# Twenty joined score stretches, key trees split by level, and a re-planned order in a sparse-attention and feed-forward kernel

## The chip, the cores and the metric

The kernel runs on one core of one Trainium2 chip. A core has five engines, each with a queue of its own that it works through in order: TensorE (PE; its weight loads are shown apart as PEld), VectorE (DVE), ScalarE (ACT), GpSimd (POOL) and SyncE (SP). Semaphores order them against each other. POOL and SP also issue DMAs. The metric is the device time of one execution in microseconds (us).

## What is computed

Chunk-selecting causal attention over 4 batches of 8 heads, 768 tokens, head size 64, followed by a feed-forward network with squared ReLU over the 3072 tokens:

```python
k_chunks = k.reshape(B, H, nc, chunk, D)              # chunk = 32, nc = 24
k_min, k_max = np.min(k_chunks, axis=3), np.max(k_chunks, axis=3)
ub = np.sum(np.maximum(q * k_min, q * k_max), axis=-1)  # a bound of each query and chunk
ub = np.where(causal, ub, -1e9)
top_chunks = np.argsort(ub, axis=-1)[..., -6:]
mask = (chunk of the key is in top_chunks) & causal
attn = softmax(where(mask, q @ k.T / 8, -1e9))
x = attn @ v                                           # 3072 x 512
h = np.maximum(x @ w_in, 0.0)                          # 3072 x 2048
out = h * h @ w_out                                    # 3072 x 512
```

## The kernel before

**The work.** Heads go in pairs: four pairs a batch, sixteen in all, numbered p from 0. The first 128 tokens of each batch attend only to themselves and are done apart (`first_attention`). For the other 640 queries (`NS` = 5 tiles of 128) each pair has two stages.

`stage_a(p)` makes the selection. For batches 0 and 1 keys and queries are transposed on PE (`turn_keys`, `turn_queries`); for batches 2 and 3 (`BY_DMA` = 2) SP does it by DMA transposes (`turn_by_dma`). DVE then takes minimum and maximum of the keys over each chunk: by one reduction (L892) for batches 0 and 1, by a tree of pairwise maxima or minima (`tree`, L857 to L883) for batches 2 and 3, two trees for two pairs. The tree halves the 32 keys of a chunk in five steps: L871 (two instructions), L877 three times, L880. PE multiplies the bounds (`ub`), DVE finds the six best of each query (L805) and marks them (`select`).

`stage_b(p)` is the attention proper. For batches 0 and 1 the marks ride along as 24 more rows of the score product (88 rows instead of 64; L1056). For batches 2 and 3 (p from `RP` = 8 on) `spread` turns the marks into a 0/1 mask: SP transposes them into `sT`, four DMAs write them to DRAM (`rowm`, L1000), four more read them back, spread over partitions, as `keep` (L1005; two buffers), and POOL cuts the diagonal (L669). `stage_b_rows` (L1099) computes these pairs' scores: the 20 tiles of one head fill five PSUM banks (`HEADS`), the two heads of a pair lie in the upper and the lower 64 rows of the array (L1139). Each bank then has an exponential on ACT (L1154), a product with `keep` on DVE (L1157) and four products with the values on PE (L1164). `normalise` divides by the sums (L726, L728) and writes x.

The feed-forward (`ffn`) runs once for the first tiles of all batches and once for each batch, between the attention of the next pairs: `up` (L1231), relu (L1238 on ACT or L1240 on DVE), square (L1252 or L1254), `down` (L1271), a copy `ob<-py` (L398 on ACT or L400 on DVE; three `ob` buffers) and the output DMA on SP (L1285).

**Stretches.** One entry of PE's queue that computes scores of batches 2 and 3 is called a stretch here. `HELD = [(0, 1), (2, 3), (4,)]` (L1027) says which banks of a pair go together: two, two and one, each for both heads. So a pair has three stretches, of four, four and two PSUM banks, and the eight pairs have 24. PSUM buffers: three of tag `ps`, one `tp`, two `av`, two `ff`; a stretch of four banks takes all of `ps` and `tp`.

**What sets the order.** Nothing is scheduled at run time. Every step is entered with `plan.op`, with its possible engines and a cost for each. `ORDER` lists, for each engine, the numbers of the steps in the order of its queue; a step that could run on two engines runs on the one whose list holds it. `Plan.order` walks through these lists with its costs, with a time that a result takes to the next engine (`HAND_OVER`, `BUSY`) and with a small model of the DMAs (`late` is added to a transfer). What comes of that walk is which buffer of a tag a tile gets, how the lists interleave as the program is written, and how many idle matmuls keep PE warm in the first 30 us (`keep_warm`). The walk's costs do not run on the chip; the lists do.

Of the kernel before, what the change touches and what calls it, by code (L numbers as in the profile page):

```python
# [78 lines left out]
class Plan:  # L79
# [7 lines left out]
    HAND_OVER = {"PE": 0.22, "ACT": 0.10, "DVE": 0.10, "POOL": 0.12, "SP": 0.1}  # L87
    BUSY = 0.09
# [27 lines left out]
    def order(self):  # L116
# [10 lines left out]
        landed, done = [], []  # L127
        dma = Transfers()
        at = {e: 0 for e in self.given}
        while len(done) < len(self.ops):  # L130
            found = []
            for engine, line in self.given.items():
# [18 lines left out]
                if op.packets and not op.turns and len(landed) >= 8:  # L151
                    st = max(st, landed[-8].end)
# [16 lines left out]
            if op.packets:  # L169
                dma.add(op)  # L170
                if not op.turns:
                    landed.append(op)
# [27 lines left out]
    def write(self):  # L200
# [47 lines left out]
        1790 1791 1796 1797 1800 1801 1802 1803 1806 1807 1808 1809""",  # L248
    "ACT": """
# [21 lines left out]
        1804 1810""",  # L271
    "DVE": """
# [1093 lines left out]
```

## Time and profile before

| | |
|---|---|
| median of 3 runs | 264.62 us (267.29, 264.62, 264.58) |
| the profiled execution | 266.55 us, its span 264.7 us |
| granted clock of PE | 1.000 |
| DMA packets, bytes | 111124, 37.92 MB |
| idle time of PE ahead of `ph` (L1231), of which most waits for `ob` (L400) | 2.8 us |
| score stretches, L1139 | 24 |
| chain that ended last, by engine | PE 64%, DVE 18%, DMA 6%, ACT 5% |

How to read the lines that follow. In a group of instructions stand line, engine, operation, tile written <- tile read, shapes, count, then busy us, the mean of one in ns, and the idle time of the engine just before, with what ended it. In a timeline stand start and duration in us; x4 means four like instructions drawn together. Matmuls overlap: a matmul's drawn end includes its way through the array, and the next one starts earlier, so the time that a matmul costs is read from start to start. In a table of stages stand the stretch of time, its length, and for PE, PEld, DVE, ACT and POOL the busy time with the count of instructions, then the granted clock, the DMA share and GB/s. SPq is SP's issuing of DMAs.

### The profile page before, as it was taken

What the parts mean: (1) busy time and instruction counts of PE and PEld (TensorE: products, weight loads), DVE (VectorE), ACT (ScalarE), POOL (GpSimd) and SP (SyncE); (2) the same over time, 40 slices, a digit from 0 to 9 for tenths busy, and PEclk for the clock granted to TensorE, in tenths of its full rate; (3) what the DMA queues carried; (4) which work ended last, traced back from release to release, by engine and by line L of the source; (5) the groups of instructions that cost most, each with busy time, mean ns of one, the idle gap of its engine ahead of it and who ended that gap; (6) DMA issues with size and microseconds to landing.
All of it is one profiled execution on the core that took longest, in us unless ns stands there. A gap on an engine that the chain in (4) does not pass through costs nothing.

```text
span 264.7 us, 6744 instructions
## 1 busy us (share of the span) xinstructions
PE 252.7 (95%) x2416; PEld 158.3 (60%) x2439; DVE 194.0 (73%) x729; ACT 186.1 (70%) x403; POOL 126.9 (48%) x209
## 2 busy tenths in 40 slices
PE   8899999999999999999999999997999999999995
PEld 5677656665767765664675545444756554765543
DVE  3799799857799899999999998836887750562220
ACT  1479899984999989865999988465977631572521
POOL 8998999599447856471286627361050000000000
PEclk9999999999999999999999999999999999999999
DMA  8999999999999999988999999979870005110023
GB/s 150 161 167 169 179 112 176 163 144 155 134 128 202 115 142 174 107 165 150 225 172 211 204 252 231 121 203 245 246 225 0 0 3 139 67 54 0 7 90 143
DMA packets 111124, 37.92 MB, mean 143 GB/s; under 512 B 98724, under 2 KB 103752, under 8 KB 111092
## 3 DMA queue, kind: packets, MB, share of 16 engines
q0 software_dynamic: 76672, 14.19, 72.7%
q1 hardware_dynamic: 34420, 23.31, 40.8%
q8 instruction: 19, 0.31, 0.5%
q14 instruction: 13, 0.11, 0.2%
HBM read 37.75 MB, written 7.60 MB: 171 GB/s over the span
## 4 chain that ended last, share of the span: by engine, by line
PE 64%; DVE 18%; DMA 6%; ACT 5%; issue 3%; SPq 1%; POOL 1%; DVEq 0%; ACTq 0%; POOLq 0%
PE py L1271 24%; PE ph L1231 23%; PE ps L1056 4%; PE ps L1139 3%; PE av L1164 3%; DMA qn<-in_q_dram 3%; PE av L1067 2%; DMA keep<-rowm 2%; ACT ht L1238 2%; DVE e L1157 2%; DVE h L1254 2%; DVE m L805 2%; DMA out_dram<-ob 1%; DVE selb L965 1%; DVE tree L877 1%
## 5 line engine op out<-in xcount | busy, mean ns | idle before, releaser
L1231 PE MATMUL ph<-xT,w_in_sb 128*128 128x256 bf16 (+2 forms) x592 | 100.1, 304 | 2.8 <-DVE ob L400 2.2
L1271 PE MATMUL py<-w_out_sb,h 128*128 128x512 bf16 (+2 forms) x377 | 89.2, 370 | 1.2
L1231 PEld LDWEIGHTS <-w_in_sb 128*128 128x128 bf16 x592 | 53.6, 97 | 28.4 <-issue 6.7
L1238 ACT ACTIVATE ht<-ph 128x384 bf16<-128x384 f32 (+2 forms) x100 | 45.5, 462 | 24.9 <-PE ph L1231 20.3
L1271 PEld LDWEIGHTS <-h 128*128 128x128 bf16 x400 | 36.3, 97 | 35.1 <-issue 1.6
L1154 ACT ACTIVATE e<-ps 128x512 bf16<-128x512 f32 x80 | 44.3, 600 | 15.0 <-PE ps L1139 12.7
L1078 ACT ACTIVATE e<-ps 128x512 bf16<-128x512 f32 x80 | 44.8, 605 | 3.2 <-PE av L1067 1.5
L1157 DVE TENSOR_TENSOR e<-e,keep 128x512 bf16<-128x512 bf16 x80 | 33.0, 444 | 5.6 <-POOL keep L669 4.5
L1240 DVE TENSOR_SCALAR ht<-ph 128x256 bf16<-128x256 f32 (+2 forms) x48 | 22.8, 476 | 19.4 <-PE ph L1231 16.4
L1252 ACT ACTIVATE h<-ht 128x256 bf16<-128x256 bf16 (+2 forms) x66 | 30.7, 478 | 5.2 <-DVE ht L1240 4.8
L669 POOL TENSOR_SCALAR_AFFINE_SELECT keep<-keep 128x256 bf16<-128x256 bf16 x40 | 18.8, 491 | 30.6 <-DMA keep<-rowm 19.4
L1254 DVE TENSOR_TENSOR h<-ht 128x256 bf16<-128x256 bf16 (+2 forms) x82 | 26.8, 334 | 9.0 <-ACT ht L1238 8.6
L1056 PE MATMUL ps<-qsc,kqc 88*128 88x384 bf16 (+2 forms) x160 | 27.5, 272 | 0.3 <-ACT e L1078 0.2
L669 POOL TENSOR_SCALAR_AFFINE_SELECT e<-e 128x128 bf16<-128x128 bf16 (+2 forms) x47 | 17.9, 397 | 19.2 <-ACT e L1078 17.4
L1000 POOL DMA_DIRECT2D rowm<-sT x24 | 15.7, 657 | 13.5 <-DMA sT<-selb 13.0
L1164 PEld LDWEIGHTS <-e 128*128 128x128 bf16 x320 | 15.7, 98 | 7.2 <-issue 1.8
L1067 PEld LDWEIGHTS <-e 128*128 128x128 bf16 x320 | 15.9, 97 | 5.6 <-DVE e L666 0.9
L398 ACT COPY ob<-py 128x512 f32<-128x512 f32 (+2 forms) x16 | 9.0, 561 | 12.6 <-PE py L1271 11.6
L1056 PEld LDWEIGHTS <-kqc 88*128 88x128 bf16 x160 | 13.2, 97 | 6.0 <-issue 0.6
L1067 PE MATMUL av<-vn,e 128*128 128x65 bf16 x240 | 16.7, 193 | 0.0
L728 DVE TENSOR_TENSOR x<-av,rc 128x320 bf16<-128x320 f32 x32 | 15.0, 479 | 0.2
L892 DVE TENSOR_REDUCE kr<-kT 128x24 bf16<-128x768 bf16 x16 | 15.0, 950 | 0.1
(108 smaller groups left out, 345.7 us busy)
## 6 DMA issues: line engine op xcount, KB each, us to landing
keep<-rowm SPq DMA_DIRECT2D x32, 320.0 KB, 4.8
out_dram<-ob SPq DMA_DIRECT2D x23, 256.0 KB, 4.5
w_in_sb<-in_moe_w_in_dram POOLq DMA_DIRECT2D x4, 512.0 KB, 6.6
w_out_sb<-in_moe_w_out_dram POOLq DMA_DIRECT2D x4, 512.0 KB, 7.6
vn<-in_v_dram POOLq DMA_DIRECT2D x15, 128.0 KB, 5.7
nt<-in_k_dram POOLq DMA_DIRECT2D x10, 128.0 KB, 5.7
nt<-in_q_dram POOLq DMA_DIRECT2D x10, 128.0 KB, 5.9
rowm<-sT POOLq DMA_DIRECT2D x24, 40.0 KB, 4.7
```

The source lines that it names most:

```text
L669: nc.gpsimd.affine_select(out=e, in_=e, compare_op=ALU.is_ge, fill=0.0, base=0, channel_multiplier=-1, pattern=[[0, n], [1, 128]])
L1056: nc.tensor.matmul(ps[:, 128 * c:128 * (c + nt)], lhsT=kqs[:, ks, hh, 128 * j:128 * (j + 1)], rhs=qss[:, ks, hh, 128 * (t0 - 1):128 * (t0 ...
L1067: nc.tensor.matmul(av[:, t - 1], lhsT=e[:, 128 * c:128 * (c + 1)], rhs=value_tile(b, h, j), start=(i == 0 and c == 0), stop=(i == len(BANK ...
L1078: nc.scalar.activation(e.tile, ps.tile, ACT.Exp, scale=scale), [sc], [ps, e])
L1154: nc.scalar.activation(e.tile, ps.tile, ACT.Exp, scale=scale), [sc], [ps, e])
L1157: nc.vector.tensor_mul(e.tile.rearrange("k (t q) -> k t q", q=128), e.tile.rearrange("k (t q) -> k t q", q=128), m[:, 4 * i:4 * i + 4, hh]),
L1164: nc.tensor.matmul(avs[hh][:, t - 1], lhsT=e[:, 128 * c:128 * (c + 1)], rhs=value_tile(b, 2 * hp + hh, j), start=(i == 0 and c == 0), stop ...
L1231: nc.tensor.matmul(ph.tile, lhsT=w_in_sb[:, ki, 128 * f:128 * (f + 1)], rhs=xT[:, c0 // 128:c1 // 128, ki], start=(ki == 0), stop=(ki == N ...
L1238: nc.scalar.activation(ht.tile, ph.tile, ACT.Relu)
L1252: nc.scalar.activation(h2[f][:, c0:c1], ht.tile, ACT.Square)
L1254: nc.vector.tensor_mul(h2[f][:, c0:c1], ht.tile, ht.tile)
L1271: nc.tensor.matmul(py.tile, lhsT=h2[f][:, 128 * t:128 * (t + 1)], rhs=w_out_sb[:, f, c0:c1], start=(f == 0), stop=(f == NFI - 1))
```

## The change

Four things are changed together.

1. `HELD` names banks of two pairs at once: five stretches of four PSUM banks for two pairs, the third of them with the last bank of the first pair and the first bank of the second. `stage_b_rows` takes two pairs, with four accumulators `av` in two buffers. There are 20 stretches.
2. Each level of a key tree is a step of its own, and there are two `tree` buffers.
3. The planner's numbers are others: hand-overs, step costs, the times of DMAs, and at most eight transfers of one queue under way, of SP's as well, where before this held for the loads alone.
4. All five lists of `ORDER` are new. PE has 580 entries where it had 584, ACT 381 where it had 402, DVE 562 where it had 510 (24 + 8 of them by the split of the trees), POOL 202 (203) and SP 115 (113). 82 keep-warm matmuls where there were 79.

```diff
-    HAND_OVER = {"PE": 0.22, "ACT": 0.10, "DVE": 0.10, "POOL": 0.12, "SP": 0.1}
-    BUSY = 0.09
+    HAND_OVER = {"PE": 0.22, "ACT": 0.15, "DVE": 0.13, "POOL": 0.12, "SP": 0.1}
+    BUSY = 0.117
...
-                if op.packets and not op.turns and len(landed) >= 8:
-                    st = max(st, landed[-8].end)
+                if op.packets and len(sent[engine]) >= 8:
+                    st = max(st, sent[engine][-8].end)
...
-"krt": 2, "tree": 1, "qp": 2,
+"krt": 2, "tree": 2, "qp": 2,
...
-            return op({"DVE": 1.63}, t0 + 5 + 2 * mm, go, got + [t_first["k", b].op] + krt_made.get(p - 1, []), [turned["k", b], kr, levels])
+            done = op({"DVE": 0.51}, t0 + 5 + 2 * mm, first, got + [t_first["k", b].op] + krt_made.get(p - 1, []),
+                      [turned["k", b], levels])
+            for i, cost in ((1, 0.265), (2, 0.17), (3, 0.122)):
+                done = op({"DVE": cost}, t0 + 5 + 2 * mm, lambda _, i=i: next_(i), [done], [levels])
+            return op({"DVE": 0.122}, t0 + 5 + 2 * mm, last, [done], [levels, kr])
...
-            [t], [sT, rowm], packets=150, turns=True, late=1.5)
+            [t], [sT, rowm], packets=150, turns=True, late=3.2)
...
-    HELD = [(0, 1), (2, 3), (4,)]
+    HELD = [((0, 0), (0, 1)), ((0, 2), (0, 3)), ((0, 4), (1, 0)),
+            ((1, 1), (1, 2)), ((1, 3), (1, 4))]
...
-    def stage_b_rows(p, x):
+    def stage_b_rows(p0, x):
...
-        avs = [buffer("av", [128, NS, D + 1], F32, name="av") for _ in range(2)]
+        avs = {(w, hh): buffer("av", [128, NS, D + 1], F32, name="av")
+               for w in range(2) for hh in range(2)}
...
-                    [xT] + xs, late=3.6))
+                    [xT] + xs, late=2.0))
...
-                packets=2 * w, turns=True)
+                packets=2 * w, turns=True, late=0.8)
...
-            stage_b(p, x)
+            if p < RP:
+                stage_b(p, x)
+            elif p % 2:
+                stage_b_rows(p - 1, x)
```

The other changed numbers are the costs of single steps on ACT, DVE and POOL (0.46 to 0.478 for an exponential, say) and `late` of the DMA transposes of keys and queries (4.5 to 2.8) and of `sT` (1.5 to 1.3).

More of the change, by code (lines that the diff above doesn't have):

```diff
@@ L126, in order @@
                 waiting.setdefault(n, []).append(op)
-        landed, done = [], []
+        sent, done = {e: [] for e in free}, []
         dma = Transfers()
@@ L170, in order @@
                 dma.add(op)
-                if not op.turns:
-                    landed.append(op)
+                sent[engine].append(op)
             for t in op.tiles:
@@ L385 @@
                  "vn": B - 1, "x": 2, "xT": 2,
-                 "rowm": 12, "kr0": 1, "keep": 2, "st": 2, "kr": 2, "krt": 2, "tree": 1, "qp": 2, "qm": 2, "ubm": 2, "m8": 2, "rc": 2}, lambda *a: keep_warm(*a), ORDER)
+                 "rowm": 12, "kr0": 1, "keep": 2, "st": 2, "kr": 2, "krt": 2, "tree": 2, "qp": 2, "qm": 2, "ubm": 2, "m8": 2, "rc": 2}, lambda *a: keep_warm(*a), ORDER)
     POOLS = {"tp": pst, "ps": pss, "av": psav, "ff": psf, "e": epool, "h2": hpool,
@@ L727, in normalise @@
             rc[:, 0:n], av[:, :, D]), [op], [av, rc])
-        return plan.op({"DVE": 0.06 + 0.00108 * D * n}, due, lambda _: nc.vector.tensor_mul(
+        return plan.op({"DVE": 0.06 + 0.00099 * D * n}, due, lambda _: nc.vector.tensor_mul(
             x(), av[:, :, 0:D],
@@ L829, in stage_a @@
             got = list(loaded["k", b])
-            kc_on, qc_on, q_on = {"DVE": 0.45}, {"DVE": 0.45}, 0.22
+            kc_on, qc_on, q_on = {"DVE": 0.45}, {"DVE": 0.45}, 0.24
         else:
@@ L835, in stage_a @@
                       [kT, nat["k", b]] + ([firsts["k"]] if p < RP else []))]
-            kc_on, qc_on = {"DVE": 0.52, "ACT": 0.78}, {"ACT": 0.70, "DVE": 0.43}
+            kc_on, qc_on = {"DVE": 0.52, "ACT": 0.72}, {"ACT": 0.655, "DVE": 0.467}
             q_on = 0.40
@@ L863, in level, with shape, first @@
                 return levels[:, at:at + 8 * NT * n].rearrange("d (x j) -> d x j", j=n)
-            def go(_):
+            def shape(i):
+                return level(i).rearrange("d (t x) j -> d t x j", t=NT)
+            def first(_):
                 for t0, t1, src in (
@@ L869, in go, with next_, last @@
                     src = src.rearrange("d t p (c j) -> d t (p c) j", j=CH)
-                    dst = level(0).rearrange("d (t x) j -> d t x j", t=NT)
-                    nc.vector.tensor_tensor(dst[:, t0:t1], src[:, :, :, 0:CH // 2],
+                    nc.vector.tensor_tensor(shape(0)[:, t0:t1], src[:, :, :, 0:CH // 2],
                                             src[:, :, :, CH // 2:], op=f)
-                src = dst
-                for i in range(1, 4):
-                    n = CH >> (i + 1)
-                    dst = level(i).rearrange("d (t x) j -> d t x j", t=NT)
-                    nc.vector.tensor_tensor(dst, src[:, :, :, 0:n], src[:, :, :, n:2 * n], op=f)
-                    src = dst
+            def next_(i):
+                n = CH >> (i + 1)
+                nc.vector.tensor_tensor(shape(i), shape(i - 1)[:, :, :, 0:n],
+                                        shape(i - 1)[:, :, :, n:2 * n], op=f)
+            def last(_):
                 src = level(3).rearrange("d (t p c) j -> d t p c j", t=NT, p=2)
@@ L890, in stage_a @@
         else:
-            r = [op({"DVE": 0.75 if first_kr else 0.865}, t0 + 5 + 2 * mm,
+            r = [op({"DVE": 0.72 if first_kr else 0.828}, t0 + 5 + 2 * mm,
                     lambda _, mm=mm, f=f: nc.vector.tensor_reduce(
@@ L954, in stage_a @@
             [um, made["ubmask"]], [ubm])
-        m = [op({"DVE": 0.071 * 2 * n}, t0 + 17 + i, lambda _, i=i, n=n: best(i, i + n),
+        m = [op({"DVE": 0.124 + 0.049 * 2 * n}, t0 + 17 + i, lambda _, i=i, n=n: best(i, i + n),
                 [um], [ubm, m8]) for i, n in ((0, 3), (3, 2))]
@@ L987, in stage_a @@
             return
-        cs = [[op({"DVE": 0.345, "ACT": 0.385}, t0 + 23 + 2 * hh,
+        cs = [[op({"DVE": 0.345, "ACT": 0.414}, t0 + 23 + 2 * hh,
                   lambda e, hh=hh, i=i: copy_selection(e, hh, i),
@@ L1009, in spread @@
                     [4 * COPIES, CH // COPIES, 256 * 5])),
-            out, [rowm, m], packets=1700, turns=True, late=1.7) for i in range(len(TILES) // 5)]
+            out, [rowm, m], packets=1700, turns=True, late=1.5) for i in range(len(TILES) // 5)]
         prepared[p, 0] = prepared[p, 1] = []
         cut = {ROW[j]: plan.op(
-            {"POOL": 0.36}, due + 2, lambda _, j=j: causal("POOL", m[:, ROW[j]], 2),
+            {"POOL": 0.43}, due + 2, lambda _, j=j: causal("POOL", m[:, ROW[j]], 2),
             [kept[ROW[j] // 5]], [m]) for j in range(1, NT)}
@@ L1076, in stage_b @@
                 scored[p].append(sc)
-                done = plan.op({"ACT": 0.46}, due + 0.5, lambda _, e=e, ps=ps:
+                done = plan.op({"ACT": 0.478}, due + 0.5, lambda _, e=e, ps=ps:
                                nc.scalar.activation(e.tile, ps.tile, ACT.Exp,
@@ L1083, in stage_b @@
                     done = plan.op(
-                        {"DVE": 0.07 + 0.065 * n, "POOL": 0.14 + 0.11 * n}, due + P["vm"],
+                        {"DVE": 0.07 + 0.065 * n, "POOL": 0.17 + 0.12 * n}, due + P["vm"],
                         lambda en, e=e, d0=d0, d1=d1: causal(
@@ L1120, in queries @@
                 "x t h d -> x t (h d)")
-        avs = [buffer("av", [128, NS, D + 1], F32, name="av") for _ in range(2)]
-        prev = [None, None]
+        avs = {(w, hh): buffer("av", [128, NS, D + 1], F32, name="av")
+               for w in range(2) for hh in range(2)}
+        prev = {}
         for n, banks in enumerate(HELD):
-            due = HALVES * p + 8 * n
+            due = HALVES * p0 + 8 * n
+            made_by = []
+            for w in sorted({w for w, _ in banks}):
+                made_by += [t_first["k", b].op] + loaded["k", b] + loaded["q", b] \
+                    if b >= BY_DMA else turned_by[p0 + w]
             tags = ["ps", "ps", "ps", "tp"]
-            pss_ = {(i, hh): buffer(tags.pop(0), [128, 512], F32, name="ps")
-                    for i in banks for hh in range(2)}
+            pss_ = {(w, i, hh): buffer(tags.pop(0), [128, 512], F32, name="ps")
+                    for w, i in banks for hh in range(2)}
             def scores(_, banks=banks, pss_=pss_):
-                for i in banks:
+                for w, i in banks:
+                    hp = (p0 + w) % NP
                     c = 0
@@ L1146, in stage_b_rows @@
             sc = plan.op({"PE": 0.105 + 0.22 * len(banks)}, due, scores,
-                         made_by + last_scores[-1:], list(pss_.values()) + homes)
+                         list(dict.fromkeys(made_by)) + last_scores[-1:],
+                         list(pss_.values()) + homes)
             last_scores.append(sc)
-            for i in banks:
+            for w, i in banks:
+                p, hp = p0 + w, (p0 + w) % NP
+                m = keep[p]
                 for hh in range(2):
-                    ps = pss_[i, hh]
+                    ps = pss_[w, i, hh]
                     e = buffer("e", [128, 512])
-                    ex = plan.op({"ACT": 0.46}, due + 0.5 + 2 * (i - banks[0]) + hh, lambda _, e=e, ps=ps:
+                    ex = plan.op({"ACT": 0.478}, due + 0.5 + hh, lambda _, e=e, ps=ps:
                                  nc.scalar.activation(e.tile, ps.tile, ACT.Exp,
                                                       scale=scale), [sc], [ps, e])
-                    mu = plan.op({"DVE": 0.334}, due + P["vm"], lambda _, e=e, i=i, hh=hh:
+                    mu = plan.op({"DVE": 0.345}, due + P["vm"], lambda _, e=e, i=i, hh=hh, m=m:
                                  nc.vector.tensor_mul(
@@ L1168, in values @@
                                 skip_group_check=True)
-                    prev[hh] = plan.op({"PE": 0.125}, due + P["va"], values,
-                                       [mu, prev[hh], made["ones", b]] + loads_of("v", b, hp),
-                                       [e, avs[hh], nat["v", b]])
-        for hh in range(2):
-            x_done[b, 1].append(normalise(
-                avs[hh], NS, lambda h=2 * hp + hh: x[:, :, D * h:D * (h + 1)],
-                prev[hh], [x], HALVES * (p + 1) + 7))
+                    prev[w, hh] = plan.op({"PE": 0.125}, due + P["va"], values,
+                                          [mu, prev.get((w, hh)), made["ones", b]]
+                                          + loads_of("v", b, hp),
+                                          [e, avs[w, hh], nat["v", b]])
+                    if i == len(HEADS) - 1:
+                        x_done[b, 1].append(normalise(
+                            avs[w, hh], NS, lambda h=2 * hp + hh: x[:, :, D * h:D * (h + 1)],
+                            prev[w, hh], [x], HALVES * (p + 1) + 7))
     last_ups, last_downs = [], []
```

35 lines of the change are left out of this document (15 added, 20 removed), and 186 rows, old and new, of the table ORDER.

## The prediction, made before the changed kernel was run

> **What bounds the kernel now.** I read the page's engine sums first, then the busy time by stage, the waits of PE, and last the timelines round the places that the change touches.
>
> ```profile
> span 264.7 us, 6744 instructions
> PE 252.7 (95%) x2416; PEld 158.3 (60%) x2439; DVE 194.0 (73%) x729; ACT 186.1 (70%) x403; POOL 126.9 (48%) x209
> ```
> ```profile
> 35.00:85.00 50.00, 48.96 (x524) 32.33 (x528) 42.29 (x145) 44.24 (x93) 37.63 (x58) 1.00 1.91 152
> 85.00:160.00 75.00, 73.21 (x762) 45.94 (x768) 71.20 (x339) 63.99 (x149) 40.74 (x71) 1.00 1.37 175
> 160.00:185.00 25.00, 22.20 (x218) 12.06 (x221) 15.62 (x45) 14.89 (x31) 11.86 (x23) 1.00 0.98 199
> 185.00:265.00 80.00, 75.93 (x578) 44.98 (x582) 38.73 (x108) 39.45 (x88) 4.25 (x10) 1.00 0.27 81
> ```
> ```profile
> PE ph L1231 <- DVE ob L400: 2.2, 1, 2.2
> PE av L1164 <- DVE x L728: 0.8, 2, 0.5
> PE av L1067 <- DVE x L728: 0.3, 1, 0.3
> ```
>
> The second fence has one stage a line: its length, then PE, PEld, DVE, ACT and POOL busy, the granted clock (1.00 throughout) and DMA. PE is the bound: 95% of the span. What a new order can win is PE's idle time: 75.00 - 73.21 = 1.8 us in 85 to 160, where DVE has only 75.0 - 71.2 = 3.8 us to spare, and 25.00 - 22.20 = 2.8 us in 160 to 185, nearly all of it one wait of 2.2 us for a copy of `ob` (third fence: total, times, longest). The rest of the span is matrix work that both kernels do alike. From 185 us on DVE and ACT are half idle: no term there.
>
> **Joined stretches (HELD).** A stretch of scores runs in 64-row tiles between work in 128-row tiles. A full one, of four banks, and a small one, of two:
>
> ```profile
> 119.62 0.59 PE L1271 MATMUL py<-w_out_sb,h 128*128 128x512 bf16 x2
> 120.15 0.45 PE L1139 MATMUL ps<-qt,k1t 64*128 64x512 bf16 x4
> 120.43 0.33 PE L1139 MATMUL ps<-qt,kt 64*128 64x384 bf16 x2
> 120.69 4.50 PE L1271 MATMUL py<-w_out_sb,h 128*128 128x512 bf16 x19
> ```
> ```profile
> 128.52 0.60 PE L1231 MATMUL ph<-xT,w_in_sb 128*128 128x256 bf16 x4
> 129.05 0.40 PE L1139 MATMUL ps<-qt,kt 64*128 64x128 bf16 x6
> 129.38 1.05 PE L1231 MATMUL ph<-xT,w_in_sb 128*128 128x256 bf16 x8
> ```
>
> The full one takes 120.69 - 120.15 = 0.54 us from its start to the next start, the small one 129.38 - 129.05 = 0.33. Ahead of both stands a gap: eight `ph` matmuls take 1.05 us with the last one's 0.3 us tail, so about 0.11 each, four 0.43, but 129.05 - 128.52 is 0.53: 0.10. So two small ones cost 2 x 0.43 = 0.86 us of PE and one joined full one 0.64. Eight small ones become four joined: 4 x 0.22 = **-0.88 us**, all on PE, where nothing hides it. Sixteen full ones stay. Bounds: nothing (PE idles elsewhere for it) and 0.88; I take 0.88, since PE is the bound. What it adds: a small stretch left the `tp` bank free, a joined one takes it, and four exponentials (600 ns each in the group that reads `ps`, quoted below) empty it in 2.4 us; in 90 us come 20 stretches, one in 4.5 us, so I cost that at nothing. If that cover is gone, the next stretch waits at most 2.4 us.
>
> **Key trees level by level.** Eight trees of five levels each were one entry of the plan, run without a break; now each level is an entry, and there are two `tree` buffers.
>
> ```profile
> 97.22 0.89 DVE L877 TENSOR_TENSOR tree<-tree 128x384 bf16<-128x384 bf16 x3
> 98.15 0.21 DVE L880 TENSOR_TENSOR krt<-tree 128x48 bf16<-128x48 bf16 x1
> 98.28 0.31 DVE L666 TENSOR_TENSOR e<-e,tri 128x128 bf16<-128x128 bf16 x1
> ```
>
> The last level starts 98.15 - (97.22 + 0.89) = 0.04 us after the level that it needs; the mask behind it, which needs nothing of it, starts at 98.28, 0.08 before 98.15 + 0.21. So a hop between levels costs 0.12 us of DVE. In the changed order of DVE 7 of the 32 hops are left with nothing between; 25 x 0.12 = -3.0 us of DVE. The work itself is unchanged.
>
> The Trainium skill, "VectorE: DVE Perf Modes", section "The DRAIN you can't avoid", speaks against this term: the next Vector op does not start until the pipe is empty, waits or not, so filling a hop would win nothing (0 in place of -3.0), though it adds that an op that is not held starts earlier. The trace sides with the exception: the 0.08 us above.
>
> **Work that changes engine.** I counted both orders. In the feed-forward of batches 0 and 1 (roughly 60 to 160 us), 5 relus and 9 squares go from ACT to DVE. In the same time DVE takes 5 copies of `sT` and gives up 3 copies of `qT`, 2 of `kT`, one of `ub` and 3 masks.
>
> ```profile
> L1154 ACT ACTIVATE e<-ps 128x512 bf16<-128x512 f32 x80 | 44.3, 600 | 15.0 <-PE ps L1139 12.7
> L1240 DVE TENSOR_SCALAR ht<-ph 128x256 bf16<-128x256 f32 (+2 forms) x48 | 22.8, 476 | 19.4 <-PE ph L1231 16.4
> L1252 ACT ACTIVATE h<-ht 128x256 bf16<-128x256 bf16 (+2 forms) x66 | 30.7, 478 | 5.2 <-DVE ht L1240 4.8
> L1254 DVE TENSOR_TENSOR h<-ht 128x256 bf16<-128x256 bf16 (+2 forms) x82 | 26.8, 334 | 9.0 <-ACT ht L1238 8.6
> ```
> ```profile
> L400 DVE COPY kqc<-kT 64x768 bf16<-64x768 bf16 x14 | 7.7, 552 | 0.3
> L400 DVE COPY qsc<-qT 64x640 bf16<-64x640 bf16 x13 | 6.3, 481 | 0.1
> L400 DVE COPY qsc<-sT 24x384 bf16<-24x384 bf16 x6 | 2.1, 351 | 0.3 <-PE sT L403 0.2
> ```
>
> DVE: 5 x 0.476 + 9 x 0.334 = +5.4; 5 x 0.351 - 3 x 0.481 - 2 x 0.552 = -0.8; the copy of `ub` and the masks, priced by the smallest copy above, 4 x 0.35 = -1.4. Net +3.2, less 3.0 from the hops: +0.2 us against 3.8 us to spare. ACT loses some 9 x 0.478 of squares and the relus. On the path: 0 (bounds: a gain of the 1.8 us that PE idles there, a loss of 3.2 if no hop is filled and nothing is spare).
>
> **The new order, where PE stops longest.** In SyncE's queue, and then the chain:
>
> ```profile
> 161.63 0.64 SPq L1000 DMA_DIRECT2D rowm<-sT  x1
> 169.17 1.21 SPq L505 DMA_TRANSPOSE sT<-selb  x1
> 170.49 0.54 SPq L1005 DMA_DIRECT2D keep<-rowm  x1
> 171.13 3.04 SPq L505 DMA_TRANSPOSE xT<-x  x2
> 174.22 0.58 SPq L1005 DMA_DIRECT2D keep<-rowm  x1
> 174.90 0.67 SPq L1000 DMA_DIRECT2D rowm<-sT  x1
> 175.67 0.39 SPq L1285 DMA_DIRECT2D out_dram<-ob  x1
> ```
> ```profile
> 175.67 3.96 DMA out_dram<-ob
> ...
> 179.73 0.70 DVE ob L400
> ...
> 180.48 0.60 PE ph L1231 x4
> ```
>
> An output waits its turn behind transposes and mask copies, lands 3.96 us later, and only then can the next copy take its `ob` slot, free the bank of `py` and let `ph` start. The new planner counts eight transfers outstanding per queue and 0.8 us more for an output; its numbers cost nothing on the chip but chose another order. There the same output stands behind sT, keep, keep, xT, xT: the `rowm` issue (0.67, with its gap 0.77) is behind it. Between the two copies that share the slot PE has one group of four `py` matmuls more than before; I do not count that, since the last values of x, for which the transposes wait, stand later in PE's queue too. So the wait shrinks by **-0.77**. Bounds: 0 and 2.17 (all of it). The two `rowm` issues that move from POOL to SyncE cost 2 x 0.67 us of a queue that idled from 161.63 + 0.64 = 162.3 to 169.2; nothing behind them waits. Three more keep-warm matmuls at the start fill idle time: 0, at most 3 x 0.11.
>
> **Sum.** -0.88 - 0.77 = -1.65. The profiled execution took 266.55 us, its span of 264.7 and 1.85 round it; it would become 264.9. It stands 1.93 above the median of the runs, 264.62; the same difference from the median gives 264.62 - 1.65 = 262.97: **263.0 us**, own range 262.0 to 264.4.
>
> **The rivals.**
> *The order is better everywhere.* The planner's errors in the hand-overs were what left PE waiting. For it: the longest wait is one that its old numbers did not see. Against: the other waits are 0.8 us and less, spread. The whole 2.17 goes: 264.62 - 0.88 - 2.17 = 261.6; the 1.8 us of 85 to 160 as well: 259.8. Middle 260.7.
> *A mask transfer comes to the open.* A joined stretch scores the first bank of a pair with the last of the pair before, so four `e` tiles wait for two `keep` buffers, the later of which may still be on its way.
>
> ```profile
> POOL keep L669 <- DMA keep<-rowm: 19.4, 8, 6.9
> ```
> ```profile
> keep<-rowm SPq DMA_DIRECT2D x32, 320.0 KB, 4.8
> ```
> POOL waits for these up to 6.9 us today, while PE has `py` and `ph` work to do. If PE's queue runs out of it once, a landing of 4.8 us is exposed: 263.0 + 4.8 = 267.8. It decides from 1.65 us of new waits on (slower than before), from 4.3 on by over 1%. Against: no wait of PE for `e<-e,keep` is in the list above.
> *DVE full.* The hops stay empty: DVE then takes 3.2 of its 3.8 us to spare, and of these 3.2 between 0 and all land on PE; middle 1.6: 264.6, no change. This is what the rule of the Trainium skill's page "VectorE: DVE Perf Modes" would make of it; the overlap of 0.08 us speaks against. If the new levels do not fill hops, the tree part also doesn't do what it says.
>
> **How the numbers follow.** Forecast 0.42, better everywhere 0.36, DVE full 0.09, a transfer in the open 0.13. About 1% (2.6 us) is what a measurement of this kernel can tell from no change: faster means below 261.97, slower above 267.27. All of "better everywhere" but little, with a tail of the forecast, gives faster 0.37; the open transfer gives slower 0.13; same is the rest, 0.50. The range runs from 259.8 (the far end of the better order) to 266.2 (DVE full at its far end, 263.0 + 3.2).
>
> **What would show it.** Twenty stretches of 0.54 us, none of 0.33, each with its gap. Five tree levels with other instructions between them, DVE busy about as before in 85 to 160 and ACT less. The wait of `ph` for the `ob` copy down to about 1.4 us: at 0 the rival was right, at 2.2 my reading of the queue was wrong. Wrong as a whole if PE waits for `keep`, or if its idle time in 35 to 85 us, of which no step speaks, changes by over 1 us.

## The result, and the profile after

The changed kernel takes 261.82 us, the median of four runs (261.13 to 262.22). The kernel before, run beside it, takes 264.60 us (263.61 to 267.29). The ratio of the two, formed over all runs, is 0.987, with an interval from 0.982 to 0.992: faster by 1.3%, where the two medians alone give 1.1%. The profiled execution took 261.63 us with a span of 259.8, against 266.55 and 264.7 before. That pair differs by 4.9 us and the medians by 2.8: the profiled execution of before was a long one, and this matters below.

First the span and engine sums, and the table of stages, with the same edges and columns as before (length, then PE, PEld, DVE, ACT, POOL busy).

```profile
span 259.8 us, 6787 instructions
PE 252.7 (97%) x2442; PEld 159.9 (62%) x2442; DVE 201.3 (78%) x749; ACT 179.1 (69%) x382; POOL 126.0 (48%) x208
```
```profile
35.00:85.00 50.00, 49.03 (x536) 32.51 (x535) 46.05 (x152) 43.47 (x88) 39.84 (x63) 1.00 1.91 151
85.00:160.00 75.00, 74.21 (x787) 47.15 (x784) 71.51 (x341) 62.01 (x139) 40.77 (x72) 1.00 1.31 177
160.00:185.00 25.00, 25.00 (x257) 14.37 (x256) 18.42 (x60) 18.23 (x39) 8.74 (x18) 1.00 1.06 220
185.00:265.00 80.00, 71.37 (x526) 41.70 (x524) 38.73 (x101) 31.72 (x73) 4.64 (x10) 0.99 0.23 72
```

PE is drawn as busy in sum as before, 252.7 us, so that all 4.9 us look like idle time of PE that is gone. By stage: 160 to 185 us had 25.00 - 22.20 = 2.80 us of it and has none, 85 to 160 had 1.79 and has 0.79, 35 to 85 had 1.04 and has 0.97. Part of that is no idle time. Before, 23 `py` matmuls have a weight load in the page but no record of their own (2416 against 2439), and each hole reads as idle time. Among the edits of the kernel before that follow, with the same matmuls, b_tree_out has none missing, and PE is busy 253.9 us; with 23 missing it is 252.2 to 252.9 (b_tree, b_out, b_same). So 1.0 to 1.7 us are only drawn as idle, about a third of that from 85 to 160 us. What PE loses is therefore read from start to start below. DVE is as full as before in 85 to 160 (71.20, now 71.51), and ACT has 2.0 us less there.

The waits of PE in the new kernel, total, times and longest:

```profile
PE wt L641 <- DVE ubmask L449: 1.1, 1, 1.1
PE py L1286 <- DVE ht L1255: 0.4, 1, 0.4
PE ub L798 <- DVE kbd L948: 0.3, 1, 0.3
```

The first lies in the start and was there before. Of `ob`, for which PE stood 2.2 us, nothing is left; no wait after the start is over 0.4 us, and none is for `keep`. SyncE's queue, where that wait came from, and then what hangs on it:

```profile
163.39 1.22 SPq L506 DMA_TRANSPOSE sT<-selb  x1
165.90 1.18 SPq L1014 DMA_DIRECT2D keep<-rowm  x2
167.75 3.48 SPq L506 DMA_TRANSPOSE xT<-x  x2
171.32 0.54 SPq L1300 DMA_DIRECT2D out_dram<-ob  x1
171.91 0.54 SPq L1014 DMA_DIRECT2D keep<-rowm  x1
172.54 1.34 SPq L1009 DMA_DIRECT2D rowm<-sT  x2
...
174.69 0.58 ACT L399 COPY ob<-py 128x512 f32<-128x512 f32 x1
175.85 0.61 PE L1246 MATMUL ph<-xT,w_in_sb 128*128 128x256 bf16 x4
```

The output is issued at 171.32 where it was 175.67. Part of these 4.35 us is PE itself, which is ahead in the new kernel: it comes to the `ph` that hung on this output at 175.85, where it was 180.48 - 2.17 = 178.31. Measured against that point the output goes out 175.85 - 171.32 = 4.53 us ahead, where it was 2.64: 1.9 us more. It passes one `keep` and one `rowm` issue, as the diff of the queues said; but the transpose `sT`, which heads this row, also starts at 163.39 where it was 169.17. What it waited for stands in the waits of SyncE's queue from 162 to 171 us, and the cause in POOL's timeline, both of the kernel before:

```profile
SPq L505 <- DMA rowm<-sT: 6.7, 1, 6.7
```
```profile
162.99 1.37 POOL L669 TENSOR_SCALAR_AFFINE_SELECT keep<-keep 128x256 bf16<-128x256 bf16 x3 [0.91 <-DMA keep<-rowm]
164.31 1.84 POOL L557 DMA_DIRECT2D vn<-in_v_dram  x2
166.13 0.44 POOL L669 TENSOR_SCALAR_AFFINE_SELECT keep<-keep 128x256 bf16<-128x256 bf16 x1
166.49 0.70 POOL L1000 DMA_DIRECT2D rowm<-sT  x1
```

The same two views of the new kernel, from 156 us on:

```profile
SPq L506 <- DMA rowm<-sT: 1.4, 1, 1.4
```
```profile
156.37 1.92 POOL L1009 DMA_DIRECT2D rowm<-sT  x3 [6.81 <-DMA sT<-selb]
```

A `rowm` transfer, which reads an `sT` buffer and so keeps it, stood in POOL's queue behind cuts of `keep` that wait for a DMA, and behind two loads; it was issued at 166.49. SyncE held the next transpose for 6.7 us for it, and everything behind that. Each `sT` is read by four such transfers, and there are two `sT` buffers. By the lists, the `sT` at 169.17 takes over the buffer of one transposed at 146.53, and the transfer at 166.49 is the last that reads it. In the new lists the transposes come in another order: the same pair's `sT`, at 163.39, takes over the buffer of one transposed at 151.24, whose four transfers, three on POOL and one on SyncE, go from 156.37 on, ahead of those cuts. Between 156 and 165 us SyncE waits 1.4 us for such a transfer. So the output lands in time, and the copy at 174.69 and `ph` behind it wait for nothing.

The end of a key tree on DVE, and what follows it:

```profile
96.42 0.47 DVE L884 TENSOR_TENSOR krt<-tree 128x48 bf16<-128x48 bf16 x1
96.82 1.01 DVE L1255 TENSOR_SCALAR ht<-ph 128x384 bf16<-128x384 f32 x2
97.75 0.31 DVE L921 TENSOR_SCALAR qp<-qt 128x640 bf16<-128x640 bf16 x1
```

The relus `ht` at 96.82, which PE needs before it can reuse a bank of `ph`, stand right behind a last level. One joined stretch of the new kernel, the third kind (last bank of one pair, first of the next), on PE:

```profile
129.85 1.03 PE L1246 MATMUL ph<-xT,w_in_sb 128*128 128x256 bf16 x8
130.81 0.39 PE L1150 MATMUL ps<-qt,kt 64*128 64x128 bf16 x6
131.04 0.38 PE L1150 MATMUL ps<-qt,k1t 64*128 64x512 bf16 x2
131.36 0.83 PE L1246 MATMUL ph<-xT,w_in_sb 128*128 128x256 bf16 x6
```

From its start to the next start it takes 131.36 - 130.81 = 0.55 us. All 20 take 0.54 to 0.55, and none of 0.33 is left.

### The profile page after: what moved, and what is told of

It is laid out like the page before. It is cut to its first block, busy times and chain, and to the rows that moved or that the text cites. A ratio compares the mean times of both kernels' runs of the same rounds, so it can differ in the third digit from the quotient of the medians.

```text
span 259.8 us, 6787 instructions
## 1 busy us (share of the span) xinstructions
PE 252.7 (97%) x2442; PEld 159.9 (62%) x2442; DVE 201.3 (78%) x749; ACT 179.1 (69%) x382; POOL 126.0 (48%) x208
## 4 chain that ended last, share of the span: by engine, by line
PE 66%; DVE 14%; DMA 7%; POOL 6%; issue 4%; ACT 2%; SPq 1%; POOLq 0%; DVEq 0%; ACTq 0%
PE py L1286 28%; PE ph L1246 22%; PE ps L1150 4%; PE ps L1064 3%; PE av L1178 3%; DMA kt<-nt 3%; DMA v<-in_v_dram 2%; DVE h L1269 2%; PE av L1075 2%; DMA nt<-in_k_dram 2%; DVE ht L1255 2%; DVE kr L901 2%; DVE e L1171 2%; POOL nt L549 1%; POOL e L670 1%
## 5 line engine op out<-in xcount | busy, mean ns | idle before, releaser
L1246 PE MATMUL ph<-xT,w_in_sb 128*128 128x256 bf16 (+2 forms) x592 | 99.1, 304 | 0.8 <-DVE ht L1255 0.2
L1286 PE MATMUL py<-w_out_sb,h 128*128 128x512 bf16 (+2 forms) x400 | 92.2, 370 | 0.4 <-DVE ht L1255 0.4
L1253 ACT ACTIVATE ht<-ph 128x256 bf16<-128x256 f32 (+2 forms) x92 | 40.2, 444 | 25.6 <-PE ph L1246 20.5
L1168 ACT ACTIVATE e<-ps 128x512 bf16<-128x512 f32 x80 | 43.4, 600 | 14.6 <-PE ps L1150 8.5
L1086 ACT ACTIVATE e<-ps 128x512 bf16<-128x512 f32 x80 | 44.3, 603 | 2.7 <-PE ps L1064 2.3
L1255 DVE TENSOR_SCALAR ht<-ph 128x256 bf16<-128x256 f32 (+2 forms) x56 | 28.3, 507 | 19.5 <-PE ph L1246 18.0
L1269 DVE TENSOR_TENSOR h<-ht 128x256 bf16<-128x256 bf16 (+2 forms) x93 | 32.0, 351 | 5.1 <-ACT ht L1253 4.6
L1267 ACT ACTIVATE h<-ht 128x256 bf16<-128x256 bf16 (+2 forms) x55 | 25.7, 479 | 6.1 <-DVE ht L1255 5.7
L670 POOL TENSOR_SCALAR_AFFINE_SELECT e<-e 128x128 bf16<-128x128 bf16 (+2 forms) x50 | 19.7, 405 | 17.1 <-ACT e L1086 16.1
L1009 POOL DMA_DIRECT2D rowm<-sT x22 | 14.3, 651 | 10.0 <-DMA sT<-selb 9.8
L399 ACT COPY ob<-py 128x512 f32<-128x512 f32 (+2 forms) x12 | 6.6, 549 | 12.6 <-PE py L1286 12.5
```

The lines of the kernel that those rows point to most:

```text
L670: nc.gpsimd.affine_select(out=e, in_=e, compare_op=ALU.is_ge, fill=0.0, base=0, channel_multiplier=-1, pattern=[[0, n], [1, 128]])
L1086: nc.scalar.activation(e.tile, ps.tile, ACT.Exp, scale=scale), [sc], [ps, e])
L1168: nc.scalar.activation(e.tile, ps.tile, ACT.Exp, scale=scale), [sc], [ps, e])
L1246: nc.tensor.matmul(ph.tile, lhsT=w_in_sb[:, ki, 128 * f:128 * (f + 1)], rhs=xT[:, c0 // 128:c1 // 128, ki], start=(ki == 0), stop=(ki == N ...
L1253: nc.scalar.activation(ht.tile, ph.tile, ACT.Relu)
L1255: nc.vector.tensor_scalar_max(ht.tile, ph.tile, 0.0)
```

## The experiments

The theory after the result had three parts: the joined stretches bring what was forecast (some 0.9 us), the `ob` wait goes whole and not by 0.77, and the split trees, forecast at nothing, let DVE hand PE its work in time between 85 and 116 us. The rival was that one part brings nearly all of it, or that the parts bring nothing one by one and only the new lists as a whole do. Times in this section are medians; each kernel ran on one chip beside the kernel before, whose median is given. Kernels whose names begin with b are edits of the kernel before, with a of the one after. Numbers in the edits are those of steps in `ORDER`.

**The kernel before once more** (b_same, nothing changed).

> The kernel before, unchanged, profiled once more. If the wait of ph for the copy of ob (2.17 us at 178 us) is part of every execution, it stands here again between 1.5 and 2.5 us. If it belongs to the one profiled execution, which was 1.9 us above the median, it is under 0.5 us here and the time is near 264.5.

It took 265.33 us beside a median of 265.09, so this execution is a usual one. Its longest wait after the start:

```profile
PE ph L1231 <- DVE ob L400: 0.8, 1, 0.8
```

The wait of 2.2 us that the prediction worked with is 0.8 us here, in the same program. Its POOL queue says why, at the place that was shown above for the longer execution:

```profile
161.45 1.43 POOL L669 TENSOR_SCALAR_AFFINE_SELECT keep<-keep 128x256 bf16<-128x256 bf16 x3
165.25 0.70 POOL L1000 DMA_DIRECT2D rowm<-sT  x1
```

There the cuts of `keep` had waited 0.91 us for a mask transfer; here they wait for none. The `rowm` behind them is issued 1.24 us earlier (165.25, was 166.49), SyncE holds `sT` for 4.9 us (was 6.7), the output goes out 1.26 us earlier (174.41, was 175.67) and lands in 3.43 us (was 3.96). So most of the difference between the two executions comes down the chain that was read above, from POOL's queue to SyncE's. It does not show what lets a mask transfer land late in one execution.

**The output issued earlier** (b_out): on SyncE's list the output that `ob` waits for moves ahead of one `keep` and one `rowm` issue.

```diff
+move("SP", 1043, 1507)
```

> The kernel before with one entry of SyncE's queue moved: the output that frees the ob slot goes ahead of one keep and one rowm issue. Theory (the terms add up): it is issued 1.3 us earlier, the wait falls from 2.2 to about 0.9 us and the kernel gains 1.3 us, 0.5%. Rival (given back): PE stops a little later for something else, and the gain is under 0.4 us.

264.54 us beside 265.09, ratio 0.998 (0.996 to 1.001). No wait for `ob` is left in its trace, and PE is busy 24.53 of the 25 us from 160 to 185 (23.79 in b_same). That execution is the fastest of its twelve, 1.1 us below their median. Here the place of one DMA issue in a queue removes the wait. In time it is worth some 0.5 us, with an interval that reaches from a gain of 1.1 to a loss of 0.3.

**The trees split, in the order of before** (b_tree): every level a step, two `tree` buffers, and steps that stood next to the tree on DVE's list put between the levels. For one tree:

```diff
+e = levels(1)
+put(614, 605, [e[0], 614, e[1], 870, e[2], 786, e[3], 605, 1057])
...
-"krt": 2, "tree": 1, "qp": 2,
+"krt": 2, "tree": 2, "qp": 2,
```

> The kernel before with the key trees alone split by level, two tree buffers, and other work or the other tree's level put between the levels. Theory: DVE is the bound from 95 to 116 us, where PE idles 0.9 us, and 30 of 32 hops of 0.12 us are filled; the kernel gains 0.8 to 1.3 us there. Rival (the rule that the pipe empties after every op): 0. Second rival (the gain after came from the new order, not from the hops): under 0.4 us.

265.11 us beside 265.09, ratio 1.000 (0.997 to 1.004). First the engine sums of b_same, then those of b_tree:

```profile
PE 252.9 (96%) x2416; PEld 158.5 (60%) x2439; DVE 194.6 (74%) x729; ACT 185.9 (71%) x403; POOL 126.9 (48%) x209
```
```profile
PE 252.2 (96%) x2416; PEld 158.6 (60%) x2439; DVE 191.5 (73%) x729; ACT 186.0 (71%) x403; POOL 127.5 (49%) x209
```

The same 729 instructions take 3.1 us less of DVE: some 0.10 us for each of the 30 hops that it was to fill, where the prediction had taken 0.12. In time this brings nothing that can be seen. What PE loses is read from start to start: the distance from one matmul to the next, less the time that its columns stream (0.216 us for 512: twenty `py` matmuls in a row from 118.33 us in the new kernel take 4.49 us, of which the last one 0.38), with the missing records taken as run. From 85 to 116 us, where no stretch stands, PE loses 2.8 us in b_same and 2.0 in b_tree, so 0.8 us reach PE there. But in this execution PE stands 1.6 us for `ob` later on, twice as long as in b_same: what is won early can be waited for again at a place whose time SyncE's queue sets. The next run tries that.

**Both of these together** (b_tree_out: the edits of b_out and b_tree).

> The kernel before with both: the output moved up in SyncE's queue, and the key trees split with other work between the levels. The wait for ob, which differs from run to run, is gone, so that the tree's part can be read. Theory (the terms add up): 0.8 us from the output and 0.8 us from the levels, 1.6 us, 0.6%. Rival (the levels win nothing by the end): as with the output alone, 0.2 to 0.4%.

264.35 us beside 265.24, ratio 0.997 (0.993 to 1.000): some 0.9 us, in the range of the rival and not told apart from nothing with certainty. PE loses 2.0 us from 85 to 116 us here too, and then waits for `ob` again:

```profile
PE ph L1275 <- DVE ob L436: 0.9, 1, 0.9
```
```profile
176.85 0.76 DVE L1201 TENSOR_TENSOR e<-e,keep 128x512 bf16<-128x512 bf16 x2 [0.65 <-POOL keep L705]
177.53 0.69 DVE L436 COPY ob<-py 128x512 f32<-128x512 f32 x1
```

This time the copy does not stand for the output: DVE comes to it straight from two products with `keep`, which POOL's cut of the mask had held up. So the two parts did not add up, and a wait at the same place had another cause.

**Joined stretches in the order of before** (b_joined): the last bank of one pair and the first of the next go into one stretch, as in the new kernel. Since a joined stretch takes `tp` as well, its exponentials had to move up on ACT's list to free the banks, and `e` got 12 buffers.

```diff
+for last in (1167, 1289, 1542, 1664):
+    ORDER["PE"].remove(last)
+for what, behind in [(1104, 1095), (1101, 1104), (1098, 1101), ...]:
+    after("ACT", what, behind)
...
-"e": 8,
+"e": 12,
```

> The kernel before with 20 joined stretches in place of 24; the exponentials of the joined banks are moved up in ACT's queue, and there are twelve e buffers instead of eight. Theory: four small stretches go at 0.42 us each and four grow by 0.21: 0.84 us less, 0.3%. Rival: the joined stretch holds four banks for longer, PE waits for them, and the kernel is the same or slower.

270.09 us beside 265.09, ratio 1.020 (1.016 to 1.024): 5 us slower. Its 20 stretches are there, but PE waits 3.4 us in all for relus of ACT, 0.8 for relus of DVE and 0.9 for an exponential. ACT and then PE round the longest wait:

```profile
137.14 2.05 ACT L1190 ACTIVATE e<-ps 128x512 bf16<-128x512 f32 x4
139.05 0.69 ACT L1274 ACTIVATE ht<-ph 128x256 bf16<-128x256 f32 x2
```
```profile
139.52 0.60 PE L1267 MATMUL ph<-xT,w_in_sb 128*128 128x256 bf16 x4 [1.91 <-ACT ht L1274]
```

Four exponentials in a row hold a relu back until 139.05; both banks of `ph` wait for it, and PE stands 1.91 us. The prediction costed the four exponentials of a joined stretch at nothing, "if that cover is gone, the next stretch waits at most 2.4 us". What waits longest here is no stretch but a `ph`: the cover is a list of ACT in which no relu that PE needs stands behind the four. The 5 us are the price of this edit as a whole, which moved some 50 exponentials on ACT's list; another way to move them was not tried.

**The kernel after once more** (a_same, nothing changed).

> The changed kernel, unchanged, as the measure for the three beside it. 261.8 us, 1.1 to 1.5% under the kernel before.

261.68 us beside 265.74, ratio 0.985 (0.980 to 0.990). PE does not wait for `ob` here either, but only just: the copy waits 0.56 us for the output's landing and ends at 175.57, and PE, which is busy until then, starts `ph` at 175.62. It is the base of the six experiments that follow. Three of them (a_split4, a_oldnum, a_treefirst) ran on another chip, where a_oldnum, at 261.87, serves as a second base.

**Every stretch in two** (a_split20): each of the 20 stretches is computed in two halves, with the next entry of PE's list between them, so there are 40.

```diff
+SPLIT = [i for i in ORDER["PE"] if i in [1112, 1125, 1138, 1155, ...]]
+for k, i in enumerate(sorted(SPLIT)):
+    line = ORDER["PE"]
+    line.insert(line.index(i) + 2, 1840 + k)
```

> The changed kernel with each of its 20 stretches computed as two of half the size, with the next entry of PE's queue between them: 40 in place of 20. Theory (each more change of the tile mode costs PE 0.21 us, and PE is the bound): 20 x 0.21 = 4.2 us more, some 266.0. Rival (the time is hidden in PE's idle time, or smaller stretches let their banks go sooner and win it back): under 2 us more.

265.80 us beside 265.74, ratio 1.002 (0.999 to 1.005); 4.1 us more than a_same, 0.21 us for each added stretch. (Drawn again at random from the runs on record, six and twelve, the difference lies between 3.4 and 5.1 us, 0.17 to 0.26 for a stretch.) One of them in its trace:

```profile
123.01 0.39 PE L1160 MATMUL ps<-qt,kt 64*128 64x256 bf16 x4
123.33 1.04 PE L1302 MATMUL py<-w_out_sb,h 128*128 128x512 bf16 x4
124.30 0.39 PE L1160 MATMUL ps<-qt,kt 64*128 64x256 bf16 x4
124.62 2.76 PE L1302 MATMUL py<-w_out_sb,h 128*128 128x512 bf16 x11
```

Each half takes 0.32 us from its start to the next, 0.64 together against 0.54 whole, and has a gap of 0.10 ahead of it: 0.20 us more in all. No wait of PE grows by more than 0.3 us, so nearly all of the 4.1 us are the halves. The Trainium skill, "TensorEngine Tiling (Array Packing)", section "Key Properties", says that a change of the tiling mode drains TensorE; it gives no price, and the 0.21 us are this kernel's price for going there and back once more.

**Four stretches in two** (a_split4): the same edit for the four joined third stretches alone (1138, 1267, 1527, 1656), which gives 24 stretches, as many as before, in the new order.

> The changed kernel with the joined third stretch of each two pairs computed as two small ones again: 24 stretches, in the new order. Theory: 4 x 0.21 = 0.8 us more, 262.5. Rival (joining also ties banks together): no difference or a gain.

262.69 us beside 265.24, ratio 0.991 (0.988 to 0.994); 1.0 us over a_same, and 0.8 over the next kernel, a_oldnum, which ran on the same chip. That is the size of the forecast's term, but the eleven runs lie from 261.88 to 265.12, and the difference is known to some 0.9 us either way. The firmer measure is a_split20.

**The planner's old numbers** (a_oldnum): the old hand-overs and transfer times (in the diff of the change, the lines with `HAND_OVER`, `BUSY` and `late`), with the new lists kept. What these can still change is which buffer a tile gets and how the lists interleave.

```diff
-    HAND_OVER = {"PE": 0.22, "ACT": 0.15, "DVE": 0.13, "POOL": 0.12, "SP": 0.1}
-    BUSY = 0.117
+    HAND_OVER = {"PE": 0.22, "ACT": 0.10, "DVE": 0.10, "POOL": 0.12, "SP": 0.1}
+    BUSY = 0.09
```

> The changed kernel with the planner's old hand-overs and old transfer times, and the new lists. The chip does not run these numbers; what they still move is which buffer a tile gets and two keep-warm matmuls. Theory: under 0.5 us of difference. Rival (the buffers that come of them matter): over 1 us slower.

261.87 us beside 265.24, ratio 0.987 (0.984 to 0.990): no difference from a_same. With the new lists kept, these numbers have no effect that can be seen. The costs of single steps and the new limit of eight transfers were not put back.

**The output issued later** (a_outlate): on SyncE's list of the new kernel the output goes behind one `keep` and two `rowm` issues.

```diff
+line.remove(1043)
+line.insert(line.index(1620) + 1, 1043)
```

> The changed kernel with the output that frees the ob slot put three entries later in SyncE's queue, behind one keep and two rowm issues. It lands in time with some 0.4 us to spare; three entries are 2.0 us. Theory: PE waits 1.5 us for the copy of ob and the kernel loses 1.5 us. Rival: the work behind it has slack and the loss is under 0.5 us.

263.92 us beside 265.74, ratio 0.992 (0.988 to 0.997); by the two ratios to the kernel before some 1.9 us over a_same. The wait is back. The execution shown took 2.3 us more than the median, its output landed only 5.16 us after its issue at 172.65, and its granted clock fell to 0.68 from 180 to 185 us, so the wait drawn is a long one:

```profile
PE ph L1254 <- ACT ob L407: 2.4, 1, 2.4
```

**Trees in one piece, late** (a_treeblock) **and early** (a_treefirst): in the new order the five levels of each tree stand together again, where the last of them stood, and where the first stood.

```diff
+for last in [1060, 1065, 1189, 1194, 1449, 1454, 1578, 1583]:
+    line = ORDER["DVE"]
+    for i in range(last - 4, last):
+        line.remove(i)
+    at = line.index(last)
+    line[at:at] = range(last - 4, last)
```

> The changed kernel with the five levels of each tree put next to each other again in DVE's queue, where the last one stood. Theory: 25 hops of 0.12 us come back, 3.0 us of DVE between 95 and 130 us; of these 0.8 to 1.3 us reach PE. Rival (DVE has enough to spare): under 0.4 us.

267.22 us beside 265.74, ratio 1.007 (1.003 to 1.010); 5.5 us over a_same, where the hops had been put at 0.8 to 1.3. DVE and then PE show why:

```profile
96.69 0.22 DVE L885 TENSOR_TENSOR tree<-k1t 128x128 bf16<-128x128 bf16 x1
96.82 0.48 DVE L885 TENSOR_TENSOR tree<-kt 128x640 bf16<-128x640 bf16 x1
97.34 1.04 DVE L890 TENSOR_TENSOR tree<-tree 128x384 bf16<-128x384 bf16 x3
98.41 0.21 DVE L895 TENSOR_TENSOR krt<-tree 128x48 bf16<-128x48 bf16 x1
98.54 1.01 DVE L1266 TENSOR_SCALAR ht<-ph 128x384 bf16<-128x384 f32 x2
```
```profile
99.14 1.14 PE L1257 MATMUL ph<-xT,w_in_sb 128*128 128x384 bf16 x6 [1.29 <-DVE ht L1266]
```

The relus that in the new kernel start at 96.82 start at 98.54, behind the whole tree of 1.9 us, and PE stands for 1.29 us of it. From 95 to 105 us PE is busy 7.62 of 10 us (9.72 in a_same). This execution is the longest of its twelve, 1.9 us over their median.

> The changed kernel with the five levels of each tree next to each other where the first one stood, instead of where the last one stood. If the hops alone cost (25 x 0.12 us of DVE), the loss is 0.8 to 1.5 us. If it was the place that cost 5.5 us in the run with the levels put last, the loss here is quite another one; if a block of 1.7 us anywhere stops the relus, it is 4 us or more again.

265.27 us beside 265.24, ratio 1.002 (0.999 to 1.004); 3.6 us over a_same and 3.4 over a_oldnum. Its waits, and ACT ahead of the first:

```profile
PE ph L1257 <- ACT ht L1264: 1.7, 2, 1.4
PE ub L809 <- DVE qp L932: 0.9, 1, 0.9
```
```profile
103.76 0.49 ACT L1264 ACTIVATE ht<-ph 128x384 bf16<-128x384 f32 x1 [1.50 <-DVE h L1280]
```

ACT's relu waited 1.50 us for a square on DVE, which stood behind a tree that ran from 100.90 to 102.80. The price does depend on where the block stands, and at both places it is well over what the hops had been put at. From 85 to 116 us PE loses 1.5 us in a_same, 4.3 here and 3.9 in a_treeblock. DVE is idle 1.7 us of that time here and 0.7 in a_same, so it is not DVE's sum alone: other work is held up behind the block. How the 3.6 and 5.5 us divide between that and the hops themselves, which also put some 2.3 and 3.9 us on DVE's total, these runs do not show.

## Why the prediction was right and wrong

The forecast was 263.0 us with a range of 259.8 to 266.2; 261.82 lies in the range, but below the likeliest case's own range of 262.0 to 264.4 and just above the 259.8 to 261.6 of the rival "better everywhere". By its own tests the rival was right: the `ob` wait is 0, and PE's idle time between 85 and 160 us shrank. The rival's reason, that the planner's better numbers made the better lists, no run here tests.

- *Joined stretches, -0.88: right.* Twenty stretches of 0.54, none of 0.33. Undoing this part alone costs 0.8 or 1.0 us (a_split4), and the price of one more stretch is 0.21 us (a_split20) against the 0.22 taken. What the step had too simple is its cover: that the four exponentials cost nothing holds in the new lists. With the one way of placing them that was tried in the old ones, the kernel lost 5 us (b_joined).
- *The `ob` wait, -0.77: the mechanism failed, and the size came near by luck.* The step reckoned that "the same output stands behind sT, keep, keep, xT, xT" and moved up only by the `rowm` issue, 0.77 us, and so left `sT` where it was; 1.4 us of wait would have stayed. Against the point where PE needs it, the output moved by 1.9 us (4.53 us ahead, was 2.64; in the two repeated executions, a_same and b_same, 5.41 and 3.51), and all of the wait went. The cause stood in the trace of before: SyncE's queue, which the prediction saw idle up to 169.2 with "nothing behind them waits", was waiting for a `rowm` that POOL had yet to issue. The two issues that move to SyncE are those of another pair; what let `sT` go is that in the new lists it follows on a buffer whose transfers POOL issues early. No run changes that alone, so that link is read from traces: before and after, and b_same, where the same `rowm` went 1.24 us sooner and the output 1.26. Putting the output back behind one `keep` and two `rowm` issues brings the wait back and some 1.9 us of time (a_outlate).
- *The size of that wait.* The prediction took 2.17 us from an execution 1.93 us above the median and subtracted a part of it from the median. In a usual execution the whole wait is 0.8 (b_same), and removing it there brings some 0.5 us (b_out). So 0.77 is about what there was to win: a third of a wait that was too long, where all of a short one went.
- *Where the other 1.2 us are.* With 0.8 for the whole wait, 0.88 for the stretches and the 1.3 to 1.4 us that PE loses less from 85 to 116 us (next point), 264.62 comes to some 261.6, and 261.82 was measured. The first two were forecast in sum, so the term that was too small by most of the 1.2 us is the one put at 0. This sum is made after the fact; no single run shows it.
- *Trees, and work that changes engine, 0 on the path: the size of DVE's term was right, its effect was not.* The hops were put at 3.0 us of DVE; splitting them in the old order took 3.1 off it (b_tree), for 30 hops, so each is some 0.10 and not 0.12. (The new list leaves 6 of the 32 empty, not 7, which alters little.) The Trainium skill's page "VectorE: DVE Perf Modes", section "The DRAIN you can't avoid", has a rule, by which the next instruction waits until the pipe is empty, and an addition, by which one that is not held starts earlier. The 3.1 us agree with the addition: instructions that do not depend on each other did fill the hops. DVE stayed as full as before in 85 to 160, as forecast (from 60 to 160 us, over which the step counted +0.2, it is 92.4 and 93.7). But the path is not untouched. From 85 to 116 us PE's starts lie closer: read as for b_tree, 2.8 us were lost before and 1.4 after (b_same 2.8, a_same 1.5). Of that, 0.8 us come with the split trees alone (b_tree), the rest with the new lists. The step looked at DVE's sum; what reaches PE hangs on what stands ahead of a relu or a square in DVE's list.
- *A transfer in the open, DVE full: neither came.* No wait for `keep`, and the hops are filled.
- *Idle time in 35 to 85 us: unchanged,* 1.04 and 0.97. Three more keep-warm matmuls, put at 0: a_oldnum, with two fewer, shows no difference.

What stays open: how much the split trees bring by themselves. In the old order PE loses 0.8 us less early on, of which nothing can be seen in the time, and a block in the new order costs 3.6 to 5.5 us; but the new order was made for split trees, so that is the price of breaking it and not the worth of the split. An order planned anew with joined stretches and whole trees would tell, and was not tried. It is also not settled why a mask transfer lands later in one execution of a program than in another, which through POOL's and SyncE's queues makes the `ob` wait 0.8 or 2.2. None of the versions tried is faster than the changed kernel.

## What to carry to other kernels

When lists of steps are made anew, a late item of a queue is late through everything ahead of it: follow the queue back to where it idled, ask what that first stop waited for and on which other queue it was issued, and see whether the change moves it in that queue's list. A term read from one execution belongs to that execution: profile the kernel twice before a wait on a transfer is taken off the median. An engine's total says whether work fits; whether it delays the bounding engine is read from what stands between a result that engine needs and its producer's queue, and a long block without a break can be dear there even where the engine has room.

## What the runs showed of the hardware

- Work of the same 729 instructions on DVE took 194.6 us with dependent ones next to each other (b_same) and 191.5 with others between (b_tree): 3.1 us.
- A change of TensorE to 64-row tiles and back costs some 0.21 us in this kernel, measured in time over 20 of them (a_split20).
- One wait for an output's landing took 0.8 us in one execution and 2.2 in another of the same program, at a granted clock of 1.00 from 160 to 185 us in both. Of the 1.4 us between them 1.26 are the later issue and 0.5 the longer landing (3.96 us against 3.43), less what PE was behind.
- The median from issue to landing of the 23 outputs on a page differs from run to run: 4.5 us in the first profile of before and 5.3 in the second, 3.3 in b_out, 2.9 after and 3.4 in a_same.
